# Second batch's keys and second block's gates moved forward, transposes in pairs, in a fused attention, gated convolution and channel mix kernel

## The chip, the cores and the metric

The kernel runs on one core of one Trainium2 chip. The metric is the time of one execution on the device in microseconds (us). It counts everything from the first load to the last store; the weights come from memory in each execution. Five engines run their own instruction streams in parallel: TensorE (PE; its weight loads are shown as PEld), VectorE (DVE), ScalarE (ACT), GpSimd (POOL) and SyncE (SP, which issues nearly all DMAs here). They wait for each other by semaphores.

## What is computed

```python
# q, k, v: (8, 8, 576, 64); x: (8, 576, 512)
q_s = exp(q - max(q, axis=-1)); q_s /= sum(q_s, axis=-1) + 1e-09     # over the head's 64 elements
k_s = exp(k - max(k, axis=2));  k_s /= sum(k_s, axis=2) + 1e-09      # over the 576 tokens
kv = einsum('bhsd,bhse->bhde', k_s, v)
x = einsum('bhsd,bhde->bhse', q_s, kv)                               # heads joined: 512 columns
gate = sigmoid(sum over 5 taps of conv_w[t] * x shifted)             # causal, within a sequence
y = (gate * (x @ w_val)) @ w_out
xk = mu_k * y + (1 - mu_k) * y_prev;  xr = mu_r * y + (1 - mu_r) * y_prev
r = sigmoid(xr @ w_r)                                                # w_r: 512 x 512
v2 = relu(xk @ w_k) ** 2 @ w_v                                       # w_k: 512 x 1024, w_v: 1024 x 512
out = r * v2
```

The weights arrive as 64-bit floats, that is as pairs of 32-bit words.

## The kernel before

The 8 x 576 tokens are cut into 12 blocks of 384. Activations lie transposed (128 of the 512 columns on the partitions, 384 tokens along the row). A block goes through 4 steps V (`pv`, product with w_val), 4 steps Y (`py`, w_out), 4 steps R (`racc`, w_r, three accumulators of 512 columns), 8 steps H (`ph`, w_k) and 8 steps A (`vacc`, w_v, three accumulators), H and A in turn. TensorE runs them one behind the other. All these products are issued in line L446 of the kernel (L449 after the change).

The first block, block 0, is computed with plain 32-bit matmuls, whose weights (`whole`) are decoded one 128 x 512 piece at a time from the words (`raw`): an activation on ScalarE (L148) and two instructions on VectorE, a shift (L149) and a shift with an or (L150). From block 1 on each product is made of three faster passes with the weights and activations split in an upper and a lower part (`wk_hi` and `lower`, `xkh` and `xkl`); the split of the weights (L237, L238) is done behind their last use in block 0. The words lie in a ring of 6 buffers on the right side of the memory (`early`, tag raw) and, for the pieces in `LEFT_WEIGHTS`, in a single buffer on the left (`first`), where a load waits for the decode of the one ahead in the list.

Beside the products of a block, the block to come is prepared: its q is loaded, normalised (`qm`, subtraction, exponential, `qs`, product: four large VectorE instructions, the first two in step `qexp`, the others in `qnorm`), transposed by TensorE (three 128 x 128 transposes into `pq`, L473), copied (`q`, or split `qh` and `ql`), multiplied with the attention's matrix (`px`), copied and split (`xf`, `xh`, `xl`) and put through the convolution for its gate (one ScalarE and four VectorE instructions for each of four column groups, then a tanh). `gf` (L582) multiplies a gate with `pv`.

The attention's matrices are made in 16 rounds, two for each of the 8 sequences, each for 4 heads: `max` (four VectorE instructions into `pm`), `turn` (two transposes into `pmT`, L318, a reduction `m`, L320), `exp` (two transposes into `mx`, L330, a subtraction and an exponential of `kt` in place) and `mm` (20 small products, `kvacc`, L344, then `den` and `kvf` on VectorE). After its `mm` a round issues the loads of k and v for the next. `kt` has one buffer. `pq`, `pmT`, `mx` and `kvacc` share two PSUM buffers (`ps_t`), `pv`, `py`, `ph`, `px` three, the accumulators three. `q`, or a pair of `qh` and `ql`, has two buffers in all.

The order of the work is written out by hand: `FRONT` is a string of step names for blocks 0 and 1 and for what is prepared beside them (`lwk1` loads piece 1 of w_k's words, `wk1` decodes it, `swk1` splits it; `x0.1` is column group 0 of the attention of block 1; `turn2` belongs to round 2, the first of the second sequence). `REST` is a table that says for blocks 2 to 11 what is put behind which of the 28 steps of a block. A tile scheduler keeps the engines' own streams nearly in that order; within a step it may move an instruction by a few places.

Of the kernel before, what the change touches and what calls it, by code (L numbers as in the profile page):

```python
# [9 lines left out]
F32R = mybir.dt.float32r  # L10
# [9 lines left out]


FRONT = (
# [13 lines left out]
).split()  # L36
REST = {
    0: "max0",
    2: "turn0",
    3: "qload",  # L40
    5: "mixk0 mm0",
    6: "qexp",
    8: "mixk1 qnorm",
    10: "max1",
    11: "mixk2 mixk3",
    12: "xturn0",
    13: "x0 turn1 xturn1",
    14: "rsig gate0",
    15: "x1 xturn2 gate1",
    17: "x2 mm1",  # L50
    18: "xturn3 gate2",
    26: "x3 gate3",
}
LEFT_GAP, RIGHT_GAP = 96, 224

START = "V0.0"
LAG = 3

CONV_ON_TENSOR = ()

LEFT_WEIGHTS = "wval1 wr0 wk1 wk5 wv2".split()


@with_exitstack
def tile_linear_attention_gated_conv_channel_mix(
# [21 lines left out]
    P = 128  # L87
# [12 lines left out]
    WC = 512  # L100
# [13 lines left out]
    behind = ctx.enter_context(tc.tile_pool(name="behind", bufs=1))  # L114
    behind.tile([P, 48], F32, name="behind_gap")

    first_ctx = ctx.enter_context(ExitStack())
    first = first_ctx.enter_context(tc.tile_pool(name="first", bufs=1))
    early_ctx = ctx.enter_context(ExitStack())
    early = early_ctx.enter_context(tc.tile_pool(name="early", bufs=1, side="right"))  # L120
    ps_acc = ctx.enter_context(tc.tile_pool(name="ps_acc", bufs=3, space=PSUM))
    ps_w = ctx.enter_context(tc.tile_pool(name="ps_w", bufs=3, space=PSUM))
    ps_t = ctx.enter_context(tc.tile_pool(name="ps_t", bufs=2, space=PSUM))
# [79 lines left out]
    raws, whole, upper, lower = {}, {}, {}, {}  # L203
# [12 lines left out]
        whole[w, at] = place(F32, "whole")  # L216
        decode(raws[n], whole[w, at])

    def open_upper(side, names):
        pool = ctx.enter_context(tc.tile_pool(name="upper_" + side, bufs=1, side=side))  # L220
        for w in names:
            _, rows, width = SHAPES[w]
            upper[w] = pool.tile([P, rows // P, width], F32R, name=f"{w}_hi")

    def split_weight(n):
        w, (kc, c0) = at = CHUNKS[n]
        if w not in upper:
            if w in ("wk", "wv"):
                first_ctx.close()
                open_upper("left", ("wk", "wv"))  # L230
            else:
                early_ctx.close()
                open_upper("right", ("wval", "wout", "wr"))
        h, t = upper[w][:, kc, c0:c0 + WC], whole[at]
        l = lower[at] = place(F32R, "lower")
        scale = 0.5 if w in HALF else 1.0
        nc.scalar.activation(h, t, AF.Copy, scale=scale)  # L237
        nc.vector.scalar_tensor_tensor(out=l, in0=t, scalar=scale, in1=f32(h), op0=ALU.mult, op1=ALU.subtract)  # L238

    def weight(i, w, kc, c0, n):  # L240

        at = w, (kc, c0 // WC * WC)
        o = c0 % WC
        if i == 0:
            return (whole[at][:, o:o + n],)
        return upper[w][:, kc, c0:c0 + n], lower[at][:, o:o + n]


    kvs = []
# [64 lines left out]
    def kv_turn(st):  # L314
        pm, n = st["pm"], HR * D // P
        pmT = ps_t.tile([P, 512], F32, tag="t", name="pmT")
        for j in range(n):
            nc.tensor.transpose(pmT[:, j * P:(j + 1) * P], pm[:, j * P:(j + 1) * P], f32(ident))  # L318
        m1 = odd.tile([P, n], F32, tag="m1", bufs=2, name="m1")
        nc.vector.tensor_reduce(  # L320
            out=m1, in_=pmT[:, :n * P].rearrange("p (j t) -> p j t", j=n), axis=AX.X, op=ALU.max
        )
        st["m1"] = m1

    def kv_exp(st):

        kt, m1, n = st["k"], st["m1"], HR * D // P
        mx = ps_t.tile([P, 512], F32, tag="t", name="mx")
        for j in range(n):
            nc.tensor.transpose(mx[:, j * P:(j + 1) * P], m1[:, j:j + 1].to_broadcast([P, P]), f32(ident))  # L330
        nc.vector.tensor_sub(
            kt, kt, mx[:, :n * P].rearrange("p (h o d) -> p h o d", o=1, d=D).to_broadcast([P, HR, NST, D])
        )
        nc.scalar.activation(kt, kt, AF.Exp)
# [134 lines left out]
    def x_turn(st, i, c):  # L469
        qt = st["qt"]  # L470
        pq = ps_t.tile([P, 512], F32, tag="t", name="pq")
        for t in range(NT):
            nc.tensor.transpose(  # L473
                pq[:, t * P:(t + 1) * P], qt[:, t, 2 * c:2 * c + 2, :].rearrange("p h d -> p (h d)"), f32(ident)
            )
        if i < 2:
            qf, = st["q", c] = (one("q", 2, "q"),)
            if i:
                nc.scalar.copy(qf, pq[:, :T])
            else:  # L480
                nc.scalar.copy(
                    qf.rearrange("c (p t) -> c p t", t=NT), pq[:, :T].rearrange("c (t p) -> c p t", t=NT)
                )
            return
        qh, ql = st["q", c] = q_pair("q")
        nc.scalar.copy(qh, pq[:, :T])
        nc.vector.tensor_sub(ql, pq[:, :T], f32(qh))

    def x_chunk(st, i, c):
        segs = segments(i)  # L490
        g = len(segs)
        px = ps_w.tile([P, 512], F32, tag="w", name="px")
        for o, n, b, s in segs:
            kv = (kvf[b],) if i < 2 else kvs[b % 2]
            passes(px[:, o:o + n], tuple(a[:, c, :] for a in kv), tuple(a[:, o:o + n] for a in st["q", c]), True, True)
        xv = padded(i, HALO, "xf", 2, "xf") if i else padded(i, HALO, "xf", NC, "xf", first)
        data = xv[:, :, HALO:]
        fill_past(i, xv, tail_x[:, c, :])
        nc.scalar.copy(data, px[:, :T].rearrange("p (g t) -> p g t", g=g))
        keep_tail(i, xv, tail_x[:, c, :])  # L500
        st["xv", c] = xv
        if i == 0:
            st["x", c] = (xv[:, 0, HALO:],)
            return
        xh, xl = st["x", c] = x_pair("x")
        gx = lambda a: a.rearrange("p (g t) -> p g t", g=g)
        nc.scalar.copy(gx(xh), data)
        nc.vector.tensor_sub(gx(xl), data, gx(f32(xh)))
# [188 lines left out]
    def rounds_of(todo, x0=0):  # L697
        out = {}
        for x, st in enumerate(todo, x0):
            out[f"max{x}"] = lambda st=st: kv_max(st)  # L700
            out[f"turn{x}"] = lambda st=st: (kv_turn(st), kv_exp(st))
            out[f"mm{x}"] = lambda st=st: (kv_mm(st), st is rounds[0] or load_round())
        return out

    def attention(i, nxt):
        out = {
            "qload": lambda: load_q(i, nxt), "qexp": lambda: q_exp(nxt), "qnorm": lambda: q_norm(nxt),
        }
        if i == 0:
            for j in range(2):  # L710
                h = slice(j * HR, (j + 1) * HR)
                out[f"qload{j}"] = lambda j=j: load_half(nxt, j)
                out[f"qexp{j}"] = lambda h=h: q_exp(nxt, h)
                out[f"qnorm{j}"] = lambda h=h: q_norm(nxt, h)
        for c in range(NC):
            out[f"xturn{c}"] = lambda c=c: x_turn(nxt, i, c)
            out[f"x{c}"] = lambda c=c: x_chunk(nxt, i, c)
            out[f"gate{c}"] = lambda c=c: x_gate(nxt, i, c)
        return out
# [79 lines left out]
```

## Time and profile before

| what | value |
|---|---|
| median of 3 runs | 821.87 us (821.69 to 822.91) |
| the profiled execution | 823.72 us, span 821.9 us |
| mean granted TensorE clock | 0.996 of full speed |
| TensorE busy | 805.6 us (98%), 4570 instructions |
| TensorE weight loads busy | 703.8 us (86%) |
| VectorE busy | 563.5 us (69%) |
| ScalarE busy | 480.6 us (58%) |
| GpSimd busy | 57.2 us (7%) |
| chain that ended last | PE 92%, DMA 3%, DVE 2%, ACT 1% |

The span is the time from the first to the last instruction of the profiled execution; its own time is 1.8 us more. A share of 98% is a mean: it hides the first 126 us, which are computed with other matmuls and with the weights still arriving, and the steady blocks behind them. A granted clock of 1.00 is 2.4 GHz, 0.50 is 1.2 GHz.

### The profile page before, as it was taken

To read this page: it belongs to the slowest core of one execution; us is meant where nothing else is said; L and a number is where in the kernel's file an instruction comes from. 1 tells how busy PE (TensorE), PEld (TensorE's weight loads), DVE (VectorE), ACT (ScalarE), POOL (GpSimd) and SP (SyncE) were. 2 spreads that over 40 slices of the span, in tenths; PEclk is the share of its full clock that TensorE was granted. 3 is DMA by queue.
4 is the path that set the end of the run, shared out by engine and by line. 5 is a ranking of instruction groups with operands and counts; after the bars stand their busy time and mean duration, and the time that the engine had idled before them with its cause. 6 is when DMAs were issued, how large, how long until landed. Compare 5 with 4: busy or idle time off the path is not lost.

```text
span 821.9 us, 12217 instructions
## 1 busy us (share of the span) xinstructions
PE 805.6 (98%) x4570; PEld 703.8 (86%) x4570; DVE 563.5 (69%) x1016; ACT 480.6 (58%) x948; POOL 57.2 (7%) x224
## 2 busy tenths in 40 slices
PE   6999989999999999999999999999999999999998
PEld 5544578998999989889899999899899998998996
DVE  7997599986758567577658578568676857653611
ACT  4677387636746654754754763763674664564542
POOL 2120011000001001000000100100000100100000
PEclk9999999999999999999999999999999999999999
DMA  9784250132142012011151211211223002000001
GB/s 316 248 284 119 59 135 1 39 97 58 32 91 72 1 39 86 12 39 55 44 97 39 59 39 39 59 39 39 59 54 82 1 1 52 27 1 13 27 1 39
DMA packets 92537, 53.25 MB, mean 65 GB/s; under 512 B 74018, under 2 KB 84286, under 8 KB 92478
## 3 DMA queue, kind: packets, MB, share of 16 engines
q1 hardware_dynamic: 92432, 52.44, 23.5%
q8 instruction: 36, 0.59, 0.3%
q14 instruction: 23, 0.19, 0.1%
q10 hardware_dynamic: 46, 0.02, 0.0%
HBM read 43.02 MB, written 9.44 MB: 64 GB/s over the span
## 4 chain that ended last, share of the span: by engine, by line
PE 92%; DMA 3%; DVE 2%; ACT 1%; issue 0%; SPq 0%; DVEq 0%; ACTq 0%
PE ph L446 24%; PE vacc L446 24%; PE racc L446 12%; PE pv L446 12%; PE py L446 12%; PE px L446 4%; PE kvacc L344 3%; PE pq L473 2%; DMA kt<-in_k_dram 1%; DMA raw<-in_moe_w_v_dram 1%; DMA dense<-in_v_dram 1%; DMA raw<-in_moe_w_k_dram 1%; DVE gate L541 1%; PE mx L330 0%; PE pmT L318 0%; DVE whole L150 0%
## 5 line engine op out<-in xcount | busy, mean ns | idle before, releaser
L446 PE MATMUL ph<-xkh,wk_hi 128*128 128x384 f32 x352 | 121.0, 344 | 0.0
L541 DVE SCALAR_TENSOR_TENSOR gate<-xf,cw,gate 128x384 f32<-128x384 f32 x192 | 117.2, 614 | 2.4
L446 PE MATMUL ph<-xkh,lower 128*128 128x384 f32 x352 | 118.4, 336 | 0.0
L446 PE MATMUL ph<-xkl,wk_hi 128*128 128x384 f32 x352 | 118.3, 336 | 0.0
L439 DVE TENSOR_TENSOR kl<-rf,kh 128x384 fp32r<-128x384 f32 x88 | 48.9, 556 | 87.8 <-ACT kh L438 86.9
L635 ACT ACTIVATE rf<-ph 128x384 f32<-128x384 f32 x96 | 47.0, 491 | 102.9 <-PE ph L446 102.5
L446 PE MATMUL vacc<-wv_hi,kh 128*128 128x512 f32 x264 | 103.9, 395 | 0.0
L446 PE MATMUL vacc<-lower,kh 128*128 128x512 f32 x264 | 103.2, 391 | 0.0
L446 PE MATMUL vacc<-wv_hi,kl 128*128 128x512 f32 x264 | 103.1, 391 | 0.0
L609 DVE SCALAR_TENSOR_TENSOR xm<-yf,mus,xm 128x384 f32<-128x384 f32 x96 | 56.6, 615 | 18.2 <-ACT xm L608 17.6
L446 PEld LDWEIGHTS ph<-xkh,wk_hi 128*128 128x128 f32 x352 | 66.2, 188 | 2.1
L446 PEld LDWEIGHTS ph<-xkh,lower 128*128 128x128 f32 x352 | 66.2, 188 | 1.9
L446 PEld LDWEIGHTS ph<-xkl,wk_hi 128*128 128x128 f32 x352 | 66.1, 188 | 0.0
L446 PE MATMUL py<-gh,wout_hi 128*128 128x384 f32 x176 | 60.8, 349 | 1.8 <-DVE gf L582 1.8
L438 ACT CAST gh<-gf 128x384 fp32r<-128x384 f32 x44 | 22.4, 510 | 65.5 <-DVE gf L582 65.5
L446 PE MATMUL pv<-xh,wval_hi 128*128 128x384 f32 x176 | 60.4, 343 | 0.0
L446 PE MATMUL pv<-xh,lower 128*128 128x384 f32 x176 | 59.8, 340 | 0.0
L446 PE MATMUL py<-gh,lower 128*128 128x384 f32 x176 | 59.4, 341 | 0.0
L446 PE MATMUL pv<-xl,wval_hi 128*128 128x384 f32 x176 | 59.4, 339 | 0.0
L446 PE MATMUL py<-gl,wout_hi 128*128 128x384 f32 x176 | 59.3, 345 | 0.0
L446 PEld LDWEIGHTS vacc<-wv_hi,kl 128*128 128x128 f32 x264 | 49.5, 188 | 10.9 <-DVE kl L439 0.3
L446 PEld LDWEIGHTS vacc<-wv_hi,kh 128*128 128x128 f32 x264 | 49.6, 188 | 8.1 <-ACT kh L438 0.3
(132 smaller groups left out, 1702.0 us busy)
## 6 DMA issues: line engine op xcount, KB each, us to landing
out_dram<-rs SPq DMA_DIRECT2D x36, 256.0 KB, 2.0
kt<-in_k_dram SPq DMA_DIRECT2D x16, 512.0 KB, 5.0
qt<-in_q_dram SPq DMA_DIRECT2D x29, 256.0 KB, 4.4
vt<-in_v_dram SPq DMA_DIRECT2D x56, 128.0 KB, 3.8
raw<-in_moe_w_k_dram SPq DMA_DIRECT2D x8, 512.0 KB, 7.3
raw<-in_moe_w_v_dram SPq DMA_DIRECT2D x8, 512.0 KB, 6.3
raw<-in_moe_w_val_dram SPq DMA_DIRECT2D x4, 512.0 KB, 6.3
raw<-in_moe_w_out_dram SPq DMA_DIRECT2D x4, 512.0 KB, 8.0
```

The lines of the kernel that those rows point to most:

```text
L344: nc.tensor.matmul(acc[e * D:(e + 1) * D, x * VW:(x + 1) * VW], lhsT=kt[:, 2 * x + e, s, :], rhs=st["v"][:, 2 * x + e, s, :], start=(s == ...
L438: nc.scalar.copy(pair[0], a)
L439: nc.vector.tensor_sub(pair[1], a, f32(pair[0]))
L446: nc.tensor.matmul(po, lhsT=left[a], rhs=right[b], start=start and x == 0, stop=stop and x == len(m) - 1)
L473: nc.tensor.transpose(pq[:, t * P:(t + 1) * P], qt[:, t, 2 * c:2 * c + 2, :].rearrange("p h d -> p (h d)"), f32(ident))
L541: nc.vector.scalar_tensor_tensor(out=gx(gate), in0=xv[:, :, HALO - sh:HALO - sh + L], scalar=tap(c, HALO - sh), in1=gx(gate), op0=ALU.mult ...
L609: nc.vector.scalar_tensor_tensor(out=gx(xf), in0=yv[:, :, 1:], scalar=mu[:, c:c + 1], in1=gx(xf), op0=ALU.mult, op1=ALU.add)
L635: nc.scalar.activation(rf, ph[:, :T], AF.Relu)
```

## The change

`turn` is split in two steps, `turn` and `exp`, and the transposes of a column group in `xturn` (into `pq`) and `xq` (the copy out of it). `FRONT` is written anew: rounds 2 and 3 are done earlier in block 0 (`mm2` behind H1 instead of H6, `mm3` behind H5 instead of A7), so are the attention of block 1 and gates 0, 1 and 3; some loads and decodes of w_v and w_k change places, and one `heat` (eight transposes of the identity) is added, which on TensorE comes ahead of the first `kvacc`. In `REST` the transposes of two column groups stand together. The upper parts of w_val, w_out and w_r get six tiles (two pieces each) in the words' ring, which is never closed, in place of a pool opened behind it. `wv2` leaves the list of the left buffer and `wk2` joins it. A strip that only shifts addresses shrinks from 96 to 32 bytes.

```diff
 FRONT = (
...
-    "Y1.0 wr1 Y2.0 wr2 Y3.0 y0.0 wk1 y1.0 y2.0 y3.0 lwv0 wk0 lwk3 lwk5 max2 R0.0 R1.0 lwk7 wr3 lwv1 lwk4 mixk0.0 lwk6 "
-    "mixk1.0 R2.0 mixk2.0 wk2 R3.0 mixk3.0 wk3 H0.0 lwv2 wv1 lwv4 lwv5 H1.0 wk4 H2.0 wk5 rsig.0 wv0 A0.0 lwv3 turn2 "
-    "H3.0 wk6 A1.0 wk7 H4.0 wv2 A2.0 wv3 H5.0 lwv6 wv4 lwv7 wv7 A3.0 H6.0 mm2 max3 A4.0 wv6 H7.0 wv5 A5.0 turn3 "
...
+    "lwk3 lwk5 R0.0 R1.0 lwk4 lwk7 wr3 mixk0.0  lwk6 mixk1.0 R2.0 mixk2.0 wk2 turn2 exp2 lwv2 R3.0 mixk3.0 wk3 H0.0 "
+    "wv1 lwv5 H1.0 wk4 lwv4 wv0 mm2 H2.0 wk5 rsig.0  qload.1 A0.0 lwv3 H3.0 wk6 wv5 max3 A1.0 wk7 H4.0 wv2 qexp.1 "
+    "turn3 exp3 A2.0 wv3 H5.0 lwv6 lwv7 mm3 qnorm.1 xturn0.1 xq0.1  wv7 A3.0 wv4 H6.0 x0.1 xturn1.1 xq1.1 gate0.1 "
...
 REST = {
     0: "max0",
-    2: "turn0",
+    2: "turn0 exp0",
...
-    12: "xturn0",
-    13: "x0 turn1 xturn1",
+    12: "xturn0 xturn1 xq0",
+    13: "x0 xq1 turn1 exp1",
     14: "rsig gate0",
-    15: "x1 xturn2 gate1",
-    17: "x2 mm1",
-    18: "xturn3 gate2",
+    15: "x1 gate1",
+    17: "xturn2 xturn3 xq2",
+    18: "x2 xq3 mm1",
+    19: "gate2",
     26: "x3 gate3",
 }
-LEFT_GAP, RIGHT_GAP = 96, 224
+LEFT_GAP, RIGHT_GAP = 32, 224
...
-LEFT_WEIGHTS = "wval1 wr0 wk1 wk5 wv2".split()
+LEFT_WEIGHTS = "wval1 wr0 wk1 wk2 wk5".split()
...
-    early_ctx = ctx.enter_context(ExitStack())
-    early = early_ctx.enter_context(tc.tile_pool(name="early", bufs=1, side="right"))
+    early = ctx.enter_context(tc.tile_pool(name="early", bufs=1, side="right"))
...
-                early_ctx.close()
-                open_upper("right", ("wval", "wout", "wr"))
+                pair = early.tile([P, 2, WC], F32R, tag="raw", bufs=6, name=f"{w}_hi")
+                upper.update({(w, kc // 2 * 2 + x): pair[:, x, :] for x in range(2)})
...
+        st["pq", c] = pq
+
+    def x_take(st, i, c):
+        pq = st["pq", c]
...
-            out[f"turn{x}"] = lambda st=st: (kv_turn(st), kv_exp(st))
+            out[f"turn{x}"] = lambda st=st: kv_turn(st)
+            out[f"exp{x}"] = lambda st=st: kv_exp(st)
```

On TensorE, round 2 stood before behind the first three `vacc` of block 0, with one `ph` between its two pairs of transposes (`x12` counts matmuls; the number behind a name tells tiles apart):

```order
L446 MATMUL racc_567<-whole,xm 128x512
L446 MATMUL ph<-xm,whole 128x384 x12
L446 MATMUL vacc_667<-whole,rf 128x512
L446 MATMUL vacc_668<-whole,rf 128x512
L446 MATMUL vacc_669<-whole,rf 128x512
L318 MATMUL pmT<-ident,pm 128x128 x2
L446 MATMUL ph<-xm,whole 128x384
L330 MATMUL mx<-ident,m_678 128x128 x2
L446 MATMUL ph<-xm,whole 128x384 x3
```

In the changed kernel the same place reads:

```order
L449 MATMUL racc_578<-whole,xm 128x512
L321 MATMUL pmT<-ident,pm 128x128 x2
L449 MATMUL racc_576<-whole,xm 128x512
L449 MATMUL racc_577<-whole,xm 128x512
L333 MATMUL mx<-ident,m_614 128x128 x2
L449 MATMUL racc_578<-whole,xm 128x512
L449 MATMUL ph<-xm,whole 128x384 x8
L347 MATMUL kvacc<-vt,kt 64x65 x20
L449 MATMUL ph<-xm,whole 128x384 x4
```

The round moved from among the `vacc` into the last `racc`, its `kvacc` from behind the fourth step A to between the `ph`.

On VectorE, round 3 (its reduction is `m_819`) came before behind the weights' splits and the end of round 2:

```order
L351 TENSOR_SCALAR den<-kvacc 128x2
L352 RECIPROCAL den<-den 128x2
L356 TENSOR_TENSOR kvf_117<-kvacc,den 64x2x64 x2
L309 TENSOR_TENSOR pm<-kt 128x256
L311 TENSOR_TENSOR pm<-pm,kt 128x256 x3
L320 TENSOR_REDUCE m_819<-pmT 128x2
L331 TENSOR_TENSOR kt<-kt,mx 128x1280
```

After the change (the reduction is now `m_781`) the normalisation of the next block's q and decodes of w_v stand between:

```order
L359 TENSOR_TENSOR kvf_117<-kvacc,den 64x2x64 x2
L417 TENSOR_REDUCE qm<-qt 128x24
L312 TENSOR_TENSOR pm<-kt 128x256
L418 TENSOR_TENSOR qt<-qt,qm 128x1536
L314 TENSOR_TENSOR pm<-pm,kt 128x256 x3
L426 TENSOR_REDUCE qs<-qt 128x24
L427 TENSOR_SCALAR qs<-qs 128x24
L428 RECIPROCAL qs<-qs 128x24
L429 TENSOR_TENSOR qt<-qt,qs 128x1536
L151 TENSOR_SCALAR raw<-raw 128x512 x2
L152 SCALAR_TENSOR_TENSOR whole<-raw 128x512
L323 TENSOR_REDUCE m_781<-pmT 128x2
```

On TensorE, the transposes of column groups 0 and 1 in a steady block (within its H steps) were two groups of three, the second behind the `mx` of a round:

```order
L446 MATMUL ph<-xkl,wk_hi 128x384
L473 MATMUL pq<-ident,qt 128x128 x3
L446 MATMUL ph<-xkh,wk_hi 128x384
L446 MATMUL ph<-xkh,lower 128x384
L446 MATMUL ph<-xkl,wk_hi 128x384
```

Now they are six in one piece:

```order
L449 MATMUL ph<-xkl,wk_hi 128x384
L476 MATMUL pq<-ident,qt 128x128 x6
L449 MATMUL ph<-xkh,wk_hi 128x384
L449 MATMUL ph<-xkh,lower 128x384
L449 MATMUL ph<-xkl,wk_hi 128x384
```

From block 1's first `racc` to the end, `pq` breaks the stream of other matmuls 37 times by itself before (three more groups stand right behind an `mx`) and 22 times after. `kvacc` is one piece of 20 in nine rounds and split into 3 and 17 by two `py` in three rounds before; it is one piece in all twelve after.

## Rows read from the trace of the kernel before

**Rows 1.** Busy time by windows; count of instructions in brackets, granted clock, DMA share, GB/s.

```profile
core 0: us, PE busy (x) PEld busy (x) DVE busy (x) ACT busy (x) POOL busy (x), PEclk, DMA share, GB/s
140.00:160.00 20.00, 19.94 (x112) 18.47 (x109) 19.82 (x38) 14.67 (x35) 2.34 (x5) 1.00 0.06 14
200.00:400.00 200.00, 200.00 (x1186) 182.54 (x1186) 138.00 (x249) 118.23 (x236) 12.93 (x55) 1.00 0.20 48
```

**Rows 2.** Waits of TensorE: us in total, times, longest.

```profile
PE py L446 <- DVE gf L582: 1.8, 1, 1.8
```

**Rows 3.** Timeline of TensorE in block 0: start, duration, work, idle before and releaser.

```profile
15.02 1.39 PE L344 MATMUL kvacc<-vt,kt 128*64 128x65 f32 x40 [0.23 <-ACT kt L334]
...
69.88 0.43 PE L330 MATMUL mx<-ident,m 128*128 128x128 f32 x2 [1.22 <-DVE m L320]
...
74.66 2.74 PE L446 MATMUL ph<-xm,whole 128*128 128x384 f32 x8
77.24 2.74 PE L446 MATMUL vacc<-whole,rf 128*128 128x512 f32 x6
...
97.53 0.41 PE L318 MATMUL pmT<-ident,pm 128*128 128x128 f32 x2 [0.57 <-DVE pm L311]
...
106.58 0.55 PE L473 MATMUL pq<-ident,qt 128*128 128x128 f32 x3
...
108.62 1.48 PE L446 MATMUL px<-q,kvf 128*128 128x192 f32 x6
109.80 0.47 PE L446 MATMUL pv<-xh,wval_hi 128*128 128x384 f32 x1
```

**Rows 4.** Windows of one microsecond behind the wait for `gf`.

```profile
122.00:123.00 1.00, 1.00 (x7) 0.96 (x7) 1.00 (x4) 1.00 (x3) 0.00 (x0) 0.88 0.00 0
123.00:124.00 1.00, 1.00 (x4) 1.00 (x4) 1.00 (x3) 1.00 (x3) 0.00 (x0) 0.50 0.00 0
...
126.00:127.00 1.00, 1.00 (x7) 1.00 (x7) 0.98 (x2) 0.77 (x2) 0.19 (x1) 0.91 0.00 0
```

**Rows 5.** Timeline of VectorE at round 3 and at the third `gf` of block 1.

```profile
95.53 0.42 DVE L309 TENSOR_TENSOR pm<-kt 128x256 f32<-128x256 f32 x1 [5.42 <-DMA kt<-in_k_dram]
...
121.14 0.55 DVE L582 SCALAR_TENSOR_TENSOR gf<-gate,pv 128x384 f32<-128x384 f32 x1
```

**Rows 6.** Timeline of TensorE in steady blocks.

```profile
191.12 0.34 PE L446 MATMUL py<-gl,wout_hi 128*128 128x384 f32 x1
...
192.98 0.34 PE L446 MATMUL py<-gh,lower 128*128 128x384 f32 x1
...
209.93 0.34 PE L446 MATMUL px<-qh,kv_hi 128*128 128x384 f32 x1
...
256.49 0.34 PE L446 MATMUL py<-gh,lower 128*128 128x384 f32 x1
...
259.16 0.33 PE L446 MATMUL py<-gh,lower 128*128 128x384 f32 x1
...
338.01 0.49 PE L473 MATMUL pq<-ident,qt 128*128 128x128 f32 x3
338.25 0.42 PE L446 MATMUL ph<-xkh,wk_hi 128*128 128x384 f32 x1
338.51 0.34 PE L446 MATMUL ph<-xkh,lower 128*128 128x384 f32 x1
338.69 0.33 PE L446 MATMUL ph<-xkl,wk_hi 128*128 128x384 f32 x1
```

**Rows 7.** VectorE by line and shape: busy, mean ns; idle before and releaser.

```profile
L423 DVE TENSOR_REDUCE qs<-qt 128x24 f32<-128x1536 f32 x11 | 19.3, 1751 | 7.0 <-ACT qt L416 7.0
L150 DVE SCALAR_TENSOR_TENSOR whole<-raw 128x512 uint32<-128x512 uint32 x28 | 18.7, 690 | 1.6 <-ACT raw L148 1.5
```

**Rows 8.** DMA issues of the page: KB each, median us from issue to landing.

```profile
kt<-in_k_dram SPq DMA_DIRECT2D x16, 512.0 KB, 5.0
...
raw<-in_moe_w_v_dram SPq DMA_DIRECT2D x8, 512.0 KB, 6.3
```

**Rows 9.** VectorE in a steady block: the subtraction behind `qh`.

```profile
208.67 0.56 DVE L487 TENSOR_TENSOR ql<-pq,qh 128x384 fp32r<-128x384 f32 x1 [4.18 <-ACT qh L486]
```

More of the change, by code (lines that the diff above doesn't have):

```diff
@@ L217, in decode_weight, with open_upper @@
         decode(raws[n], whole[w, at])
-    def open_upper(side, names):
-        pool = ctx.enter_context(tc.tile_pool(name="upper_" + side, bufs=1, side=side))
-        for w in names:
+    def open_upper():
+        pool = ctx.enter_context(tc.tile_pool(name="upper", bufs=1))
+        for w in ("wk", "wv"):
             _, rows, width = SHAPES[w]
-            upper[w] = pool.tile([P, rows // P, width], F32R, name=f"{w}_hi")
+            t = pool.tile([P, rows // P, width], F32R, name=f"{w}_hi")
+            upper.update({(w, kc): t[:, kc, :] for kc in range(rows // P)})
     def split_weight(n):
         w, (kc, c0) = at = CHUNKS[n]
-        if w not in upper:
+        if (w, kc) not in upper:
             if w in ("wk", "wv"):
                 first_ctx.close()
-                open_upper("left", ("wk", "wv"))
+                open_upper()
             else:
-                early_ctx.close()
-                open_upper("right", ("wval", "wout", "wr"))
-        h, t = upper[w][:, kc, c0:c0 + WC], whole[at]
+                pair = early.tile([P, 2, WC], F32R, tag="raw", bufs=6, name=f"{w}_hi")
+                upper.update({(w, kc // 2 * 2 + x): pair[:, x, :] for x in range(2)})
+        h, t = upper[w, kc][:, c0:c0 + WC], whole[at]
         l = lower[at] = place(F32R, "lower")
@@ L245, in weight @@
             return (whole[at][:, o:o + n],)
-        return upper[w][:, kc, c0:c0 + n], lower[at][:, o:o + n]
+        return upper[w, kc][:, c0:c0 + n], lower[at][:, o:o + n]
     kvs = []
@@ L716, in attention @@
             out[f"xturn{c}"] = lambda c=c: x_turn(nxt, i, c)
+            out[f"xq{c}"] = lambda c=c: x_take(nxt, i, c)
             out[f"x{c}"] = lambda c=c: x_chunk(nxt, i, c)
```

21 rows, old and new, of the table FRONT are left out of this document.

## The prediction

> **What bounds the kernel now.** I read the windows first. In steady blocks TensorE is busy 200.00 of 200 us while VectorE has 62 us to spare [rows 1], so a microsecond there is won only by giving TensorE less to do, or the same in fewer pieces. At the front it is otherwise: the list of waits shows where TensorE stands still, and its largest entry but for the start-up is the wait of `py` for VectorE's `gf`, 1.8 us [rows 2]. The timeline of TensorE in block 0 then gives the places [rows 3]: 0.23 us before the first `kvacc`, 1.22 us before `mx` of key round 2 at 69.88, 0.57 us before `pmT` of round 3 at 97.53. At its end comes a stretch with nothing else on TensorE: from `pq` at 106.58 to the first `pv` at 109.80 it does four groups of work (six transposes, eight `px`) in 3.22 us. The clock by windows is the last view [rows 4]: after the wait for `gf` the granted clock is 0.88, 0.50 and (two windows like the second lie between) 0.91, so the engine runs at 1.2 instead of 2.4 GHz.
>
> **The change, part by part.** On VectorE, ScalarE, GpSimd and the DMA queue the same instructions run in another order; TensorE gets one `heat` (eight transposes) more. So the sum is of waits moved and of pieces joined.
>
> 1. *Round 2 earlier.* `turn2` now stands inside the last `racc`, three `racc` (not one `ph`) apart from `mx` in the table of rows. The 1.22 us go [rows 3], if VectorE's `m` comes before its `mx`. It stands behind four decodes now, one of a word tile (wk2) whose load waits for wk1's decode. Low end of a new wait nothing, high end the old 1.22; I take nothing, as two `racc` lie between.
>
> 2. *Round 3 earlier.* The 0.57 us at 97.53 go. In exchange `m` of round 3 now stands behind the whole normalisation of the next block's q and two decodes (second pair of listings). Counted from the start of round 2's `kvacc`: on VectorE, 1.39 for `kvacc`, 5.0 until kt lands (its one buffer is read by that `kvacc`, so SP starts the load behind it) [rows 3, 8]; then `pm` 0.42 [rows 5], subtract 1.75, three `pm` 1.26, the sum over q 1.75 with 0.64 of mean idle for ScalarE's exponential ahead of it (7.0 us in 11), product 1.75 (I take the sum's duration for all three), two shifts and `m`, which I take to be as long as a `pm`, 1.26, one decode 0.69 [rows 5, 7]: 15.9, less about 0.08 for each of ten instructions that overlap their neighbour, so 15.1. On TensorE until `mx`: `kvacc` 1.39, twelve `ph`, seven `vacc`, `pmT` 0.24. Four `ph` take 2.58 from 74.66 to 77.24, so one 0.645, and a `vacc` of 512 columns 512/384 of that, 0.86 [rows 3]: 15.4. A tie. I take 0.4 of wait; low end 0, high end 3 if the words of wv6, queued on SP behind kt and five loads of v, land late. Their load takes 6.3 from issue [rows 8]; issued some 6 after `kvacc` they land at 12.3, and are wanted at 13.
>
> 3. *Attention of block 1 among block 0's `vacc`.* The 3.22 us at 106.58 hold about 2.1 of work: eight `px` at 0.197 (six take 1.18 from 108.62 to 109.80) and six transposes at 0.08 (0.24 for three at 338.01) [rows 3, 6]. So 1.15 go. The four groups of `pq` and of `px` now break into the `vacc` and `ph` of block 0 instead: 0.09 for each group of `pq` as below, 0.3.
>
> 4. *Gates 0, 1 and 3 of block 1 before its `pv`.* `gf` began at 121.14 because VectorE did the gate's multiply-adds and the next round's `pm` in turn ahead of it [rows 5]. With twelve of sixteen of them already done, two products are free at once; the third stands behind one 1.75 us reduction of q. I take 0.4 left of 1.77, bounds 0 and 1.77 [rows 2, 5]. Without the long wait the low clock does not come: 0.12 + 3 x 0.50 + 0.09 = 1.71 [rows 4].
>
> 5. *Behind that* `racc` and `ph` of block 1 come sooner, and their casts stand on ScalarE behind an exponential of round 4. Low end nothing, high end the nearest row, the 1.8 of [rows 2]; I take 0.8, since VectorE is busy 19.82 of 20 us from 140 on [rows 1].
>
> 6. *The extra heat.* Eight transposes at 0.08 to 0.09 are 0.7 us before the first `kvacc`, which waited 0.23 anyway [rows 3, 6]: 0.47 later, kept, as TensorE has work without a gap from there on; ends 0 (if the exponential is late) and 0.95 (if the half clock covers them).
>
> 7. *Steady blocks, transposes two by two.* Three `pq` take 0.24 until the next `ph`, and that `ph` 0.26 until the following one, which takes 0.18 to its successor (338.01, 338.25, 338.51, 338.69) [rows 6]. So a break of the stream costs 0.08 to 0.09 beside its transposes. The order has 37 breaks for `pq` alone before and 22 after: 15 x 0.087 = 1.3.
>
> 8. *`kvacc` no longer split.* In three blocks two `py` stood inside the 20 products of `kvacc`. Split, 256.49 to 259.16 is 2.67 with four `py` at 0.175, so 1.97; whole, 191.12 to 192.98 is 1.86 with two, so 1.51 [rows 6]. 3 x 0.46 = 1.4.
>
> 9. *Upper parts in the words' ring, wider by one raw tile for wk2, the strip of 32 bytes*: addresses only. Each pair waits for a word tile whose decode the new order places at least three steps earlier, so nothing; if one is late, its cost is a wait of at most the 0.4 to 1.8 above.
>
> Gains 1.22 + 0.57 + 1.15 + 1.37 + 1.71 + 1.3 + 1.4 = 8.7; costs 0.4 + 0.3 + 0.8 + 0.47 = 2.0; net 6.7. The profiled run took 823.72, so it would take 817.0; the median shown is 1.85 below that run, hence **815.1 us**.
>
> Two rules of the Trainium skill bear on items 2 and 4. Its page "TensorE: Matmul & The Clock Gate", part 1, "What's actually happening", says that an idle array drops to 1.2 GHz and wins 2.4 GHz back only by being busy. The trace agrees: full clock up to the 1.77 us wait, half behind it [rows 2, 4]. The same page, "Architectural detail", says that VectorE's and ScalarE's queues are strictly first in, first out. That speaks against this change: `m` cannot pass the q normalisation ahead of it. By the first rule a wait left before `py` brings the 1.71 back, by the second the tie of item 2 becomes a wait; both are among the rivals.
>
> **Rivals.**
> A, *the front's waits return elsewhere*: `m` of round 3 late by up to 3, or `py` again waiting 1.8 with the clock falling (1.37 + 1.71 lost). For it: the tie in item 2 and the load with 0.7 to spare. Against: VectorE stood idle 5.42 us before 95.53 [rows 5], time which the new order fills. Gives 821.87 - 6.7 + 3 = 818.2.
>
> B, *VectorE gives it all back*: if the 19.82 of 20 [rows 1] means that it was already the bound from 100 to 160, items 1 to 4 only bring TensorE sooner to the same wait; 2.7 of items 7 and 8 less the 0.47 of heat remain: 819.6. Against: `racc` of block 1 follows `py` without a wait in the list.
>
> C, *slower*: in steady blocks the pair of transposes holds both PSUM buffers and the copies of q, and the first `px` waits. Now the subtraction of its lower part starts at 208.67, ends at 209.23, and `px` starts at 209.93 [rows 6, 9]: 0.70 to spare. Three transposes more, if the copy waits for all six, take 0.24 of it. From a delay of 0.70 + 6.7/18 = 1.07 in each of 18 pairs the kernel is slower; with 1.2 it gives 821.87 - 6.7 + 18 x 0.5 = 824.2. Against: each group has its own tile, and the copy of the first need not wait for the second.
>
> D, *nothing to see*: A and part of B together, 820.2 to 823.5; the bound of 0.2% (1.6 us) is about what a measurement can tell.
>
> **Chances and range.** Forecast (812 to 817.5) 0.62, A 0.15, B 0.05, more gain than this 0.03, C 0.06, D 0.09. Front and steady terms are apart, so low ends of the costs give 815.1 - 2 - 0.4 = 812.7 and with all of items 5 and 6 wrong about 811. The range 811 to 819.7 holds forecast, A and B. Faster by over 0.2%: 0.81; within 0.2%: 0.10; slower: 0.09.
>
> **What would show it.** TensorE without a wait at `mx` of round 2 and with at most 0.5 at that of round 3; no window at 0.50 behind the start-up; the first `pv` of block 1 near 106.5 instead of 109.80 and the last block reached about 6 earlier; `kvacc` in one piece; six `pq` in 0.5 and no wait of a `px` in the steady blocks. It is wrong if the list of waits shows `mx` or `px` with whole microseconds, a new stretch of half clock, or blocks that take as long as before from one `racc` to the next.

## The result, and the profile after

The changed kernel took 813.38 us (median of 4 runs, 813.15 to 815.67) against 822.1 for the kernel before in the same runs: ratio 0.9902, 95% interval 0.9889 to 0.9916. That is 8.7 us less; 6.7 were forecast, and the time lies in the range.

Span and busy times on the page of the changed kernel:

```profile
span 810.9 us, 12243 instructions
PE 797.9 (98%) x4578; PEld 701.3 (86%) x4578; DVE 565.2 (70%) x1016; ACT 479.0 (59%) x948; POOL 59.9 (7%) x224
```

The waits of its TensorE, us in total, times, longest:

```profile
PE heat L738 <- DVE ident L158: 3.3, 1, 3.3
PE pmT L321 <- DVE pm L314: 2.3, 1, 2.3
PE mx L333 <- DVE m L323: 1.2, 1, 1.2
PE racc L449 <- ACT yf L607: 0.9, 1, 0.9
```

The wait of `py` [rows 2] is gone. The one at `mx` is a new one of the same size: it belongs to round 3, not to round 2. The timeline of TensorE in block 0 shows round 2 (55.01 and 56.95, no idle time) and round 3:

```profile
49.76 5.42 PE L449 MATMUL racc<-whole,xm 128*128 128x512 f32 x12 [0.91 <-ACT yf L607]
55.01 0.38 PE L321 MATMUL pmT<-ident,pm 128*128 128x128 f32 x2
...
56.95 0.38 PE L333 MATMUL mx<-ident,m 128*128 128x128 f32 x2
...
77.60 0.38 PE L321 MATMUL pmT<-ident,pm 128*128 128x128 f32 x2
...
80.01 0.43 PE L333 MATMUL mx<-ident,m 128*128 128x128 f32 x2 [1.17 <-DVE m L323]
...
84.67 1.39 PE L347 MATMUL kvacc<-vt,kt 128*64 128x65 f32 x40
...
107.60 0.74 PE L449 MATMUL pv<-xh,wval_hi 128*128 128x384 f32 x1
```

The first `pv` of block 1 comes 2.2 us sooner than in [rows 3]. From there the windows have neither idle time nor low clock, where [rows 4] had 0.50:

```profile
119.00:120.00 1.00, 1.00 (x8) 1.00 (x7) 1.00 (x1) 0.00 (x0) 0.00 (x0) 1.00 0.00 0
120.00:121.00 1.00, 1.00 (x8) 0.96 (x8) 1.00 (x4) 0.72 (x1) 0.00 (x0) 1.00 0.00 0
121.00:122.00 1.00, 1.00 (x9) 1.00 (x8) 1.00 (x3) 1.00 (x2) 0.00 (x0) 1.00 0.00 0
```

The first `racc` of the third block and of the last mark the steady stretch (nine blocks); the first `ph` ends the third block's R stage. Before:

```profile
197.02 0.39 PE L446 MATMUL racc<-wr_hi,xrh 128*128 128x512 f32 x1
...
205.44 0.34 PE L446 MATMUL ph<-xkh,wk_hi 128*128 128x384 f32 x1
...
776.16 0.39 PE L446 MATMUL racc<-wr_hi,xrh 128*128 128x512 f32 x1
```

After:

```profile
190.70 0.39 PE L449 MATMUL racc<-wr_hi,xrh 128*128 128x512 f32 x1
...
198.88 0.34 PE L449 MATMUL ph<-xkh,wk_hi 128*128 128x384 f32 x1
...
765.41 0.39 PE L449 MATMUL racc<-wr_hi,xrh 128*128 128x512 f32 x1
```

So 6.3 us were won ahead of the stretch in these two profiles, and 4.4 within it (579.14 to 574.71). The profiled run of before was a long one (823.72 against a median of 822.1); the sum of the two spans' differences is therefore more than the medians give. The second number is what does not fit: two terms were to give it, 1.3 for joined transposes and 1.4 for whole `kvacc`, together 2.7. The trace of the changed kernel speaks against the first at once:

```profile
266.29 0.82 PE L476 MATMUL pq<-ident,qt 128*128 128x128 f32 x6
266.87 0.42 PE L449 MATMUL ph<-xkh,wk_hi 128*128 128x384 f32 x1
267.13 0.34 PE L449 MATMUL ph<-xkh,lower 128*128 128x384 f32 x1
```

Six transposes take 0.58 until the next `ph`, and that one again 0.26. Two groups of three took 2 x 0.24 and each had a `ph` of 0.26 behind it [rows 6]: 0.58 + 0.26 against 2 x (0.24 + 0.26) less the 0.17 of one plain `ph`, 0.84 against 0.83. What did become shorter is the R stage: from the first `racc` to the first `ph` it takes 8.17 to 8.18 us in every block from block 2 on where it took 8.42 before (one 8.41), though no instruction in it changed. It holds three passes; their mean durations by line and shape after the change:

```profile
L449 PE MATMUL racc<-lower,xrh 128*128 128x512 f32 x132 | 51.5, 390 | 0.0
L449 PE MATMUL racc<-wr_hi,xrh 128*128 128x512 f32 x132 | 51.5, 390 | 0.0
L449 PE MATMUL racc<-wr_hi,xrl 128*128 128x512 f32 x132 | 50.9, 391 | 0.0
```

What did change are addresses: the strip of 64 bytes less moves everything on the left side of the memory (lower parts of the weights, the activations `xr`), and the upper part of w_r has a new place on the right.

### The profile page after: what moved, and what is told of

Its sections match the earlier page's. It is cut to its first block, busy times and chain, and to the rows that moved or that the text cites. A ratio compares the mean times of both kernels' runs of the same rounds, so it can differ in the third digit from the quotient of the medians.

```text
span 810.9 us, 12243 instructions
## 1 busy us (share of the span) xinstructions
PE 797.9 (98%) x4578; PEld 701.3 (86%) x4578; DVE 565.2 (70%) x1016; ACT 479.0 (59%) x948; POOL 59.9 (7%) x224
## 4 chain that ended last, share of the span: by engine, by line
PE 93%; DVE 4%; DMA 2%; ACT 0%; issue 0%; DVEq 0%
PE vacc L449 24%; PE ph L449 24%; PE pv L449 13%; PE py L449 12%; PE racc L449 11%; PE px L449 3%; PE kvacc L347 2%; PE pq L476 2%; DVE whole L152 1%; DMA raw<-in_moe_w_v_dram 1%; DMA raw<-in_moe_w_k_dram 1%; PE heat L738 1%; DVE raw L151 0%; PE mx L333 0%; PE pmT L321 0%; DVE gate L548 0%
## 5 line engine op out<-in xcount | busy, mean ns | idle before, releaser
L494 DVE TENSOR_TENSOR ql<-pq,qh 128x384 fp32r<-128x384 f32 x40 | 22.2, 556 | 62.0 <-ACT qh L493 62.0
```

## The experiments

Theory A is the prediction's steady term (joined transposes and whole `kvacc`, addresses without effect). Theory B says that the strip's 64 bytes shortened the R stages, theory C that the new place of the upper part of w_r did.

**The strip alone, in the kernel before.**

```diff
-LEFT_GAP, RIGHT_GAP = 96, 224
+LEFT_GAP, RIGHT_GAP = 32, 224
```

> The kernel before with the strip of 96 bytes cut to 32 and nothing else; every engine's order is the same. Theory A (the prediction: the strip is addresses only, the steady gain is from joined transposes and whole kvacc) expects no change, 822.1 us. Theory B (the 64 bytes are what shortens the racc of the steady blocks) expects each R stage from block 2 on at 8.17 instead of 8.42 us, so about 2.7 us less, and up to 4 with the V and Y stages: 818 to 819.5. Theory C (the new place of the upper part of w_r, in the words' ring, is what shortens racc) expects no change.

818.94 us, ratio 0.9948 (0.9932 to 0.9964). R stages of 8.17 from block 2 on; the steady stretch 575.68, 3.46 less. The third block's R stage:

```profile
195.73 0.39 PE L446 MATMUL racc<-wr_hi,xrh 128*128 128x512 f32 x1
...
203.90 0.34 PE L446 MATMUL ph<-xkh,wk_hi 128*128 128x384 f32 x1
```

That is theory B; A's "addresses only" and C fall.

This kernel shows something else. Its `py` waits as long as in [rows 2], but the windows behind that have the full clock:

```profile
PE py L446 <- DVE gf L582: 1.8, 1, 1.8
```

```profile
122.00:123.00 1.00, 0.85 (x5) 0.81 (x6) 1.00 (x4) 1.00 (x3) 0.00 (x0) 1.00 0.00 0
123.00:124.00 1.00, 1.00 (x7) 1.00 (x7) 1.00 (x3) 1.00 (x3) 0.00 (x0) 1.00 0.00 0
124.00:125.00 1.00, 1.00 (x9) 0.96 (x8) 1.00 (x2) 0.81 (x3) 0.00 (x0) 1.00 0.00 0
```

Block 1's Y stage takes 10.88 here and 12.46 in the profile of before: the 1.7 of [rows 4] are not a fixed price of that wait.

**The strip wide again, in the changed kernel.**

```diff
-LEFT_GAP, RIGHT_GAP = 32, 224
+LEFT_GAP, RIGHT_GAP = 96, 224
```

> The changed kernel with the strip back at 96 bytes, every engine's order as in the changed kernel. Theory A and theory C expect 813.4 us as the changed kernel. Theory B expects the R stages back at 8.42 us, so 816 to 817.5.

817.57 us, ratio 0.9932 (0.9918 to 0.9946); the changed kernel's is 0.9902 and, in its control below, 0.9893. R stages of 8.41 to 8.42, the steady stretch 577.99. The passes by line and shape:

```profile
L449 PE MATMUL racc<-lower,xrh 128*128 128x512 f32 x132 | 52.4, 397 | 0.0
L449 PE MATMUL racc<-wr_hi,xrh 128*128 128x512 f32 x132 | 52.4, 397 | 0.0
L449 PE MATMUL racc<-wr_hi,xrl 128*128 128x512 f32 x132 | 51.2, 393 | 0.0
```

Both passes with `xrh` are 7 ns longer. Theory B again.

**The new table alone, in the kernel before.** `turn`, `exp`, `xturn` and `xq` are split as in the change, the front keeps its order.

```diff
-    12: "xturn0",
-    13: "x0 turn1 xturn1",
+    12: "xturn0 xturn1 xq0",
+    13: "x0 xq1 turn1 exp1",
...
-    17: "x2 mm1",
-    18: "xturn3 gate2",
+    17: "xturn2 xturn3 xq2",
+    18: "x2 xq3 mm1",
+    19: "gate2",
```

> The kernel before with the new table for blocks 2 to 11 alone (transposes in pairs, kvacc whole); the front, the strip and the places of the weights as before. Theory A expects 1.3 us from the joined transposes and 1.4 from kvacc: 819.4 us. Theory B (six transposes in one piece cost what two pieces of three cost) expects only the kvacc part, 1.0 to 1.4: 820.7 to 821.1.

820.94 us, ratio 0.998 (0.9969 to 0.9990), 1.7 less by the medians; the steady stretch 577.94, 1.20 less. The interval reaches to 2.5 us less, just short of the 2.7 of A; the stretch, with 1.20, stands with B. (B in this expectation and the next is the theory that joining the transposes gains nothing.)

**Pairs taken apart, in the changed kernel.**

```diff
-    12: "xturn0 xturn1 xq0",
-    13: "x0 xq1 turn1 exp1",
+    12: "xturn0 xq0",
+    13: "x0 xturn1 xq1 turn1 exp1",
...
-    17: "xturn2 xturn3 xq2",
-    18: "x2 xq3 mm1",
+    17: "xturn2 xq2",
+    18: "x2 xturn3 xq3 mm1",
```

> The changed kernel with its pairs of transposes taken apart again in the table, kvacc left whole (44 pieces of three on TensorE instead of 20 of six). Theory A expects 18 breaks more at 0.087 us: 1.3 to 1.6 us more, 814.8. Theory B expects no change beyond 0.3 us: 813.4.

812.08 us, ratio 0.9869 (0.9851 to 0.9888). The timeline gives the steady stretch:

```profile
190.19 0.39 PE L449 MATMUL racc<-wr_hi,xrh 128*128 128x512 f32 x1
...
764.87 0.39 PE L449 MATMUL racc<-wr_hi,xrh 128*128 128x512 f32 x1
```

574.68 against 574.71 with the pairs. Joining is worth nothing in these blocks, and by elimination the 1.2 of the table are whole `kvacc`.

**The changed kernel as control, on the chip of the two runs that follow.**

> The changed kernel as it is, as a control on the chip of the runs beside it. Both theories expect a ratio to the kernel before of 0.987 to 0.991 and R stages of 8.17 us.

812.59 us, ratio 0.9893 (0.9875 to 0.9910), R stages 8.17 to 8.18. The first `pv` of block 0 begins at 21.90 here and at 20.58 in the first profile of the same kernel: the start alone moves by over 1 us from run to run.

**Which operand's address: only what lies behind the weights' pieces moved.**

```diff
     wts.tile([P, LEFT_GAP // 4], F32, name="left_gap")
+    kvp.tile([P, 16], F32, name="kv_gap")
```

> The changed kernel with 64 bytes put between the weights' pieces and the activations: the lower parts of the weights keep their addresses (0 modulo 128), the activations and the attention's matrices behind them move to 64 modulo 128, as in the kernel before. Theory B1 (it is the address of the lower parts of the weights that made racc slow) expects 8.17 us for an R stage and the time of the control. Theory B2 (it is the address of the activations) expects 8.42 and 3 to 4 us more than the control.

The places of the tiles are those of the built program, taken modulo 128 (what is left of the address in bytes when it is divided by 128). In the changed kernel lower parts, upper parts and `xr` all stand at 0; in the kernel before, lower parts and `xr` at 64 and the upper part of w_r at 0. Here the lower parts stay at 0 and all behind them moves to 64.

817.75 us, ratio 0.9952 (0.9939 to 0.9964). R 8.38 to 8.41, and the H and A stages of a block 0.16 to 0.21 longer (36.66 to 36.71 where the changed kernel has 36.50, in blocks 4, 7 and 10, which have no round in H and A). By itself this run speaks for B2, the address of the activations.

**Only the weights' pieces moved.** The same gap with the strip at 96: the lower parts at 64, all behind them at 0.

> The changed kernel with a strip of 96 bytes and 64 bytes behind the weights' pieces: the lower parts stand at 64 modulo 128 as in the kernel before, all behind them at 0 as in the changed kernel. Theory B1 expects R stages of 8.42 us and 3 to 4 us more than the control, theory B2 8.17 and the control's time. If both this and its sister are in between, it is the two together.

817.43 us, ratio 0.9950 (0.9937 to 0.9963). R 8.32 to 8.33, H and A 36.70 to 36.71. So it is neither operand alone: an R stage took 8.17 only where lower parts, activations and the upper part on the right all stand at 0 modulo 128.

**All on the left at 32.**

```diff
-LEFT_GAP, RIGHT_GAP = 32, 224
+LEFT_GAP, RIGHT_GAP = 64, 224
```

> The changed kernel with a strip of 64 bytes: lower parts and activations on the left at 32 modulo 128, the upper part of w_r on the right at 0 as ever. If a step of 64 bytes is what counts (32 as good as 0) R stages take 8.17 us and the time is that of the changed kernel. If operands must agree modulo 128, R takes 8.3 to 8.4 us and the kernel 3 to 4 us more, while the H and A stages, whose weights and activations lie together on the left, keep their time.

817.79 us, ratio 0.9938 (0.9924 to 0.9951). R 8.39, H and A 36.51. The upper part of w_r on the right, at 0, no longer agrees with the rest, at 32; both parts of w_k and w_v, on the left, still agree with each other. That fits an agreement of addresses modulo 128, and speaks against steps of 32 or 64 bytes. For H and A the common place itself does not matter: 36.52 with both parts at 64 (the kernel before), 36.51 at 32, 36.50 at 0. For R no run has a common place other than 0, so "all agree" and "all at 0" are not told apart there. Nor is 128 told from 256: where the operands of R, H and A agree modulo 128 in these runs, they agree modulo 256 as well.

The Y stage does not follow the rule modulo 128. With the activations moved (two experiments above) its upper parts, lower parts and activations `gh` all stand at 0, and it takes 8.57 in block 10:

```profile
698.94 0.33 PE L450 MATMUL py<-gh,wout_hi 128*128 128x384 f32 x1
...
707.51 0.39 PE L450 MATMUL racc<-wr_hi,xrh 128*128 128x512 f32 x1
```

The changed kernel, with `gh` at 64, takes 8.48:

```profile
695.44 0.33 PE L449 MATMUL py<-gh,wout_hi 128*128 128x384 f32 x1
...
703.92 0.39 PE L449 MATMUL racc<-wr_hi,xrh 128*128 128x512 f32 x1
```

The profiled run of the strip of 64 bytes took 819.75, the longest of its five. Its `mx` of round 3 waited longer than in any other profile, and the clock fell behind that wait, from 81.5 to 85 us:

```profile
81.13 0.43 PE L333 MATMUL mx<-ident,m 128*128 128x128 f32 x2 [1.93 <-DVE m L323]
```

```profile
82.00:83.00 1.00, 1.00 (x3) 0.42 (x2) 1.00 (x2) 0.75 (x2) 0.00 (x0) 0.50 0.00 0
```

**The added heat taken out.**

```diff
-heat3 heat0 heat7
+heat3 heat7
```

> The changed kernel without the added heat. The prediction (0.47 us of cost, kept to the end) expects 0.5 us less. The rival that the trace of the changed kernel suggests (kvacc began at 14.92 with the heat and 15.02 without it, so it waits for the exponential and the heat fills a wait) expects no change, or 0.5 to 1.5 us more if the heat keeps the clock up in the first 20 us.

812.01 us, ratio 0.9872 (0.9859 to 0.9886), not told apart from the control. Its list of waits has `kvacc` waiting 0.7 us for the exponential:

```profile
PE kvacc L347 <- ACT kt L337: 0.7, 1, 0.7
```

That `kvacc` begins at 14.96, with the heat at 14.92. So the heat fills a wait and its cost is too small to measure, and it keeps no clock up either (1.00 from 0 to 20 us in both profiles).

**The old list of the left buffer.**

```diff
-LEFT_WEIGHTS = "wval1 wr0 wk1 wk2 wk5".split()
+LEFT_WEIGHTS = "wval1 wr0 wk1 wk5 wv2".split()
```

> The changed kernel with wv2 instead of wk2 in the left buffer of words, as before the change. The prediction costs the place of wk2 at nothing and expects no change. The rival (the order of the loads of w_k and w_v decides when the decodes ahead of round 2 and round 3 come) expects other waits at mx and racc in block 0, 0.5 to 1 us either way.

811.45 us, ratio 0.9867 (0.9853 to 0.9880), the lowest of all. The interval touches the control's, not that of the first measurement. But the run without the added heat, on the same chip and with wk2 in its new place, has 811.71 to 812.38 where this one has 810.86 to 812.47. Two waits of TensorE behind the start:

```profile
PE mx L333 <- DVE m L323: 0.3, 1, 0.3
PE px L449 <- ACT q L488: 0.2, 1, 0.2
```

No `racc` waits for `yf`, but that is so without the heat and with the pairs apart as well, where wk2 keeps its new place. What no other profile with this order of the front has is so short a wait at `mx`: 0.3, against 0.8 to 1.9 in the eight others. From block 0's first `ph` to the first `pv` of block 1 it takes 48.18, against 49.2 to 49.7 in seven of them (and 52.02 in the one whose clock fell). So wk2's place likely costs 0.5 to 1 us at `mx`. That rests on one profile; the times do not show it.

**Two versions against the waits that are left.** First, wk1's decode behind the last `y` of block 0 and `mx` of round 3 behind the next step A:

```diff
-lwv1 y0.0 wk1 y1.0 max2 y2.0 y3.0
+lwv1 y0.0 y1.0 max2 y2.0 y3.0 wk1
...
-turn3 exp3 A2.0
+turn3 A2.0 exp3
```

> The changed kernel with two steps moved in the front: the decode of wk1 behind the last y of block 0, and the second half of round 3 (its mx) behind the next step A. If the waits of 0.9 us before racc (for yf, which stood behind that decode on ScalarE) and of 1.2 us before mx of round 3 are real costs of the new order, 1 to 2 us less than the control. If the order behind them only waits for something else that comes as late (words of w_v, the exponential before kvacc), no change within 0.5.

813.47 us, ratio 0.9902 (0.9885 to 0.9918): nothing won. The wait moved to `kvacc`:

```profile
PE kvacc L334 <- ACT kt L324: 1.8, 1, 1.8
```

Then, with wk1 as there, the first half of round 3 earlier still and its `mm` a step later (against the changed kernel):

```diff
-wk7 H4.0 wv2 qexp.1 turn3 exp3 A2.0 wv3 H5.0 lwv6 lwv7 mm3 qnorm.1
+wk7 turn3 H4.0 wv2 qexp.1 A2.0 exp3 wv3 H5.0 lwv6 lwv7 qnorm.1
...
-A3.0 wv4
+A3.0 mm3 wv4
```

> The changed kernel with wk1's decode behind the last y of block 0, the first half of round 3 one step earlier, its mx behind the next step A and its kvacc behind step A3 instead of H5. If the 1.2 to 1.8 us that TensorE waited at mx (or at kvacc, when only mx was moved) are a chain on VectorE and ScalarE that other work can cover, neither waits and the kernel takes 1 to 2 us less than the changed kernel: ratio to the kernel before 0.986 to 0.988. If VectorE has no time to spare there, the wait turns up later, at pq, px or py, and the ratio stays at 0.989 to 0.990.

813.28 us, ratio 0.9889 (0.9875 to 0.9902): again the control's. Now `px` waits for the copy of `q`:

```profile
PE px L436 <- ACT q L473: 1.2, 1, 1.2
```

In both the wait turned up at the next place in the chain, as the second half of each expectation has it.

## Why the prediction was right, and where it was not

The time and its sign were right, the size in part by luck. One term that the prediction put at nothing, the strip, brought 3.7 us, and one of 1.3, joined transposes, brought nothing. Without the strip the change gains 5.1 (the wide strip's 817.57 below 822.64), where 6.7 were forecast. By the medians of the experiments the 8.7 to 9.1 us are made up of: strip 3.7 (822.64 to 818.94), table 1.7 (822.64 to 820.94), front and new places of the weights 3.4 (the 5.1 less the table's 1.7; items 1 to 6 forecast 4.0). That is 8.8. The intervals of the strip (3.0 to 5.6) and of the table (0.8 to 2.5) leave about 1 us to each part.

- *Item 7, joined transposes, 1.3.* Wrong. The 0.087 behind a group was read as the price of a break and multiplied by the breaks saved; it holds for the break, but the second three transposes take 0.34 instead of 0.24, so the pair loses what it saves. The rows of before had no six in a row among fast passes, and 0.24 was taken for both halves. Taking the pairs apart changed the steady stretch by 0.03 us.
- *Item 8, whole `kvacc`, 1.4.* Right in kind; 1.2 in the steady stretch of the table alone, which holds three such places.
- *Item 9, "addresses only", nothing.* The step that failed most. It took the shift of the left side for one without effect on time. The strip is worth 3.7 us: 0.25 in each of ten R stages (2.5), the rest in the V and Y stages, which are 0.04 to 0.12 shorter each. For wk2's place nothing is shown by the times; one profile makes 0.5 to 1 us of wait at `mx` likely.
- *Items 1, 3 and 4, the front's waits.* Right in kind. Round 2 has no wait (two `racc` lie between its `pmT` and `mx`, as the end of item 1 has it, not three), the stretch without cover at 106.58 is gone, and so is all of the wait at `py` (0.4 was left to it). The low clock's 1.71 was counted in full, but it is no fixed price of that wait: the profiles of the kernel before and of the table alone have both, that of the strip alone kept the wait and lost no clock.
- *Item 2, round 3.* The wait was called a tie and taken at 0.4; it is 1.2 and 1.3 in two profiles of the changed kernel, 0.8 to 1.9 in six others with the same order of the front and the same list of the left buffer. Counted from the start of round 2's `kvacc` at 63.28, TensorE was ready for `mx` at 78.84 (80.01 less the wait), 15.6 later; the working had 15.4. But `m` ended at 79.95, 16.7 later instead of 15.1. The timeline of VectorE shows where the 1.6 came from. Nearly one half is `den`, which the working left out: it came 3 us behind the end of `kvacc`, as decodes ahead of it waited for words, and the reduction over q behind it held VectorE until `pm` began, 0.7 after `kt` had landed (69.8):

```profile
63.52 0.43 DVE L151 TENSOR_SCALAR raw<-raw 128x512 uint32<-128x512 uint32 x1 [1.85 <-DMA raw<-in_moe_w_v_dram]
...
65.79 1.90 DVE L152 SCALAR_TENSOR_TENSOR whole<-raw 128x512 uint32<-128x512 uint32 x3 [0.29 <-ACT raw L150]
67.61 0.15 DVE L354 TENSOR_SCALAR den<-kvacc 128x2 f32<-128x2 f32 x1
...
70.49 0.42 DVE L312 TENSOR_TENSOR pm<-kt 128x256 f32<-128x256 f32 x1
...
75.91 0.18 DVE L427 TENSOR_SCALAR qs<-qs 128x24 f32<-128x24 f32 x1
76.13 0.30 DVE L428 RECIPROCAL qs<-qs 128x24 f32<-128x24 f32 x1
76.46 1.76 DVE L429 TENSOR_TENSOR qt<-qt,qs 128x1536 f32<-128x1536 f32 x1
78.14 0.76 DVE L151 TENSOR_SCALAR raw<-raw 128x512 uint32<-128x512 uint32 x2
78.81 0.69 DVE L152 SCALAR_TENSOR_TENSOR whole<-raw 128x512 uint32<-128x512 uint32 x1
79.53 0.42 DVE L323 TENSOR_REDUCE m<-pmT 128x2 f32<-128x256 f32 x1
```

  The first `pm` began 7.2 after the start of `kvacc` instead of 6.4, and from there it took 9.5 to the end of `m` instead of 8.7. This other half is in the chain itself: the two small instructions on `qs` were left out (0.5), and the overlaps, taken at 0.8, come to about 0.2; the idle time for the exponential, 0.24 instead of 0.64, gives some of it back. `pmT` was done at 78.0 (77.60 and 0.38), and `m` still stood behind two shifts and a decode until 79.53. That is the strict queue of the Trainium skill's page "TensorE: Matmul & The Clock Gate" ("Architectural detail"), which the trace agrees with here.
- *Item 5, 0.8 behind block 1's V and Y.* Too much: no wait; the R stage of block 1 takes 8.57 with a group of `pq` in it. The wait for `yf` at block 0's first `racc` (0.9 and 0.7 in the two profiles of the changed kernel) is no price of the change: the kernel before has it with 0.4, with the narrow strip 0.8, and two profiles with the order of the change have none.
- *Item 6, the heat, 0.47.* Nothing that the run without it shows.
- *Rivals.* A happened in part: 1.2 and 1.3 at `mx` with full clock in the changed kernel's profiles, but 1.9 with 1.7 us lost to the clock in that of the strip of 64 bytes, which has the same order. B did not: the gain of the front was still there at block 1's `racc`. C did not: no steady `px` waits in the list. D did not: the interval of the ratio ends at 0.9916. Why one more microsecond can't be had at round 3 the last two runs show: the wait goes to `kvacc`, then to `px`.

What stays open: which matmul of a stage pays for disagreeing addresses and why, and why the Y stage goes the other way; the passes with `xrh` are longer in the kernel with the wide strip, but with the activations or the weights moved alone the lengthening spreads over all three. The parts of the front have no runs of their own either: what items 1, 3 and 4 are worth is read from waits that are gone, and only their sum with the new places of the weights, 3.4, is measured.

## What to carry to other kernels

When an edit shifts addresses, give that shift a run of its own before any reordering is credited or blamed; here a strip of 64 bytes was worth 3.7 us, as much as the new front (3.4) and more than the new table (1.7). A break in a stream of matmuls is priced by the whole piece in its new size, not by the pieces of before. And a wait that is moved out of one place in a chain of three engines must be followed to the next reader before it is booked as gained.

## What the runs showed of the hardware that was not expected

- A stage of 36 matmuls with 512 columns (R) took 8.17 us when its weights' upper and lower parts and its activations all stood at 0 modulo 128 bytes, 8.42 with the upper part at 0 and the others at 64, 8.32 to 8.41 with the lower parts or the activations alone at 64, 8.39 with both at 32 and the upper part at 0.
- The H and A stages took 36.50 to 36.53 when the two parts of their weights agreed (at 0, 32 or 64) and 36.66 to 36.71 when they did not. The activations `xkh` of H stood 64 bytes off the weights wherever these agreed, so what they count is not shown. The Y stage took 8.48 with its activations 64 bytes off and 8.57 with all at 0.
- Six transposes in a row between such passes took 0.58 us until the next matmul, three took 0.24.
- One and the same wait of 1.8 us at `py` was followed by 1.2 GHz in the profiles of the kernel before and of the table alone (a mean of 0.94 and 0.93 of full speed from 100 to 126), and by full clock in that of the strip alone. A wait of 1.93 at `mx` was followed by 1.2 GHz too.
